# Compressive memory of a four-layer attention kernel, kept as two row halves of four heads each

## The chip, the core and the metric

The kernel runs on one core of one Trainium2 chip. The metric is the device time of one execution in microseconds (us). A core has five engines with queues of their own that meet only through semaphores: TensorE (PE, with its weight loads shown apart as PEld), VectorE (DVE), ScalarE (ACT), GpSimd (POOL) and SyncE (SP), which issues most DMA transfers. Matrix products read SBUF and write banks of PSUM.

## The reference, cut to what matters

Four layers alternate over a sequence of 2048 tokens, width 512, 32 heads of 16: A (linear attention with a learned feature map), B (local attention in four segments of 512 tokens, plus a memory carried from segment to segment), A, B. The change lies in B's memory.

```python
for s in range(N):                                   # N = 4 segments
    qs, ks, vs = q[:, :, s], k[:, :, s], v[:, :, s]
    logits = einsum("bhqd,bhkd->bhqk", qs, ks) * scale + mask
    a_dot = einsum("bhqk,bhkd->bhqd", softmax(logits), vs)
    pq = phi(qs)                                     # phi(t) = t + 1 if t > 0 else exp(t)
    num = einsum("bhld,bhde->bhle", pq, M)
    den = einsum("bhld,bhd->bhl", pq, z)[..., None] + 1e-6
    outs.append(g * num / den + (1.0 - g) * a_dot)   # g = sigmoid(beta), one per head
    pk = phi(ks)
    M = M + einsum("bhld,bhle->bhde", pk, vs)
    z = z + einsum("bhld->bhd", pk)
```

`M` is 16 x 16 for each head and `z` one column of 16. The kernel keeps both side by side as 17 columns (`VW` = 17), the last one being `z`.

## The kernel before, in words

**Layer B in chunks and steps.** A segment `s` is worked in four chunks `c` of eight heads (128 rows of features). Each chunk is two halves `m` of four heads, and each `m` takes five steps, so a layer has 160 steps `k`. A step emits, in this order: the logits of `attend` (tile `lg`, two row halves of 64 at array position (64e, 0), line 1096), the logits for the row maxima in `maxima` (tiles `mx` and `my`, row halves too, line 1054), then what earlier steps put off, with the weighted sums `pv` in two of five steps, and last the words of a table.

**The tables.** `FIRST`, `GAPS`, `LAST` and `FINAL` (lines 52 to 101) say by hand which work stands in which step: `4.1` is step 1 of half 4 of a segment. `a1` is the first generator step of `memory` for chunk 1 (the read), `t1` and `m1` its transposition and its sum; `max` is `put_maxima` (a transposition of the maxima into a bank, a copy `mt` by ACT, and a DMA into row 63 of Q); `fin` transposes the weighted sums `U` and normalises them; `q`, `k`, `v`, `out` are projections of 12 products of 128x512. A `+` means the next segment, `~` that the low part is put off to a later step. PE's program order is exactly the order of emission (`held`, line 173), and so is that of DVE, ACT, POOL and SP, save for a few instructions.

**Banks.** All of these write the tile `g`, of which there are three banks (`G` = 3, line 33). A bank is used again when its last reader is done.

**The memory.** For a chunk, `acc` and `kn` are 128 rows by 8 heads x 17 columns: every row of features against all eight heads, of which only the head's own block counts. `kn` is `acc` times the 0/1 pattern `bdB` and the gate (both on POOL). The read (`a`, from segment 1 on) takes two generator steps of two products each: `ph` (512 tokens) as weights in 128x128 pieces, `kn` as the moving 128x136, then `weigh` on DVE: add 1e-6, reciprocal, multiply. The sum (`m`, up to segment 2) takes four accumulated products of 128x128 weights `pk` with 128x136 of `v`, and DVE adds the bank to `acc`. Each product in plain f32 runs as two passes, each with a weight load of its own: 4 reads are 8 passes.

The read happens for 3 segments x 4 chunks x 2 layers = 24 times, and so does the sum.

Of the kernel before, what the change touches and what calls it, by code (L numbers as in the profile page):

```python
# [7 lines left out]
F32 = mybir.dt.float32  # L8
# [9 lines left out]
DH = 16  # L18
P = 128
NSEG = 4  # L20
NC = D // P
NT = T // P
VW = DH + 1
# [9 lines left out]
G = 3  # L33
# [17 lines left out]

FIRST = """
0.1 max k2/2       | 0.2 v3/2          | 0.3 k2~
0.4 v3             | 1.1 max m0 q3/2   | 1.3 fin q3~       | 1.4 t1 k3/1
2.1 max m1 k3      | 2.3 fin ln~       | 2.4 ln~ ln~
3.3 fin q0+/2      | 3.0 w
3.1 max ln~        | 3.4 q0+~ t2
4.1 max k0+/2 load | 4.3 fin k0+/1     | 4.4 k0+ m2
5.0 n              | 5.3 fin q1+/2 n
5.1 max v0+        | 5.4 q1+~ t3  # L60
6.1 max a0+ v1+    | 6.2 n             | 6.3 a0+ fin k1+/2
6.4 k1+ m3         | 7.0 n             | 7.2 n
7.1 max q2+~       | 7.3 fin v2+/2 n   | 7.4 v2+ t0+
"""
GAPS = """
0.2 n              | 0.3 a1 fin v3/3 n
0.1 max a1 k2~     | 0.4 v3 turn~ m0
1.0 n              | 1.2 n
1.1 max q3~        | 1.3 fin out/2     | 1.4 out t1 turn~
2.1 max a2 m1 k3~  | 2.3 fin ln out/3  | 2.4 out turn~ ln  # L70
3.1 max ln ln out~ | 3.3 a2 fin q0+/2  | 3.4 q0+~ t2
4.1 max k0+~ a3 turn~ load | 4.3 a3 fin out/3 | 4.4 out~ m2
5.0 n              | 5.3 fin v0+/2 n N
5.1 max q1+~ begin | 5.4 v0+ t3
6.0 N              | 6.1 max a0+ k1+~  | 6.2 n
6.3 a0+ fin v1+/3 N | 6.4 v1+ m3       | 7.0 n N
7.1 max q2+~       | 7.2 n N           | 7.3 fin v2+/2 n N
7.4 v2+ t0+
"""

LAST = """
0.1 max a1 k2~     | 0.2 n             | 0.3 a1 fin v3/3 n
1.0 n              | 0.4 v3 turn~      | 1.2 n
1.1 max q3~        | 1.3 fin out/2     | 1.4 out turn~
2.1 max k3~        | 2.3 fin a2 out/2  | 2.4 out a2 turn~
3.1 max ln~ ln~    | 3.3 fin out/2 ln~ | 3.4 out ln~ turn~
4.1 max v/2        | 4.3 fin out/2     | 4.4 out v
5.1 max v/2        | 5.3 fin v         | 5.4 a3 pre
6.1 max v/2        | 6.3 fin v a3      | 6.4 v/2 pt~
7.1 p v pt~        | 7.3 fin v/2 p pt  | 7.4 v p pt  # L90
"""
FINAL = """
0.1 max k2~        | 0.3 fin v3/3      | 0.4 v3 a1
1.1 max a1 q3/2    | 1.3 fin q3~       | 1.4 turn~
2.1 max k3/2       | 2.3 fin k3        | 2.4 out/2
3.1 max a2 out turn~ | 3.3 fin out/2   | 3.4 out~ a2
4.1 max a3 turn~   | 4.3 fin out/2     | 4.4 out/1 a3
5.1 max out turn~  | 5.3 fin out/2     | 5.4 out/1 pre
6.1 max out~       | 6.3 fin           | 6.4 pt~
7.1 p pt~          | 7.3 fin p pt      | 7.4 p pt  # L100
# [7 lines left out]
def interleave_kernel(ctx, tc, x_in, a_wqkv, a_wphi, a_wo, b_wq, b_wk, b_wv, b_wo, b_beta,  # L108
                      c_ident, c_mask, c_bd, out):
    nc = tc.nc  # L110
    MUL, ADD, SUB, MAX, MIN = ALU.mult, ALU.add, ALU.subtract, ALU.max, ALU.min

    cp = ctx.enter_context(tc.tile_pool(name="cp", bufs=1))
    wp = ctx.enter_context(tc.tile_pool(name="wp", bufs=4))
    hp_ = ctx.enter_context(tc.tile_pool(name="hp", bufs=2))
    sp = ctx.enter_context(tc.tile_pool(name="sp", bufs=2))
# [7 lines left out]
    def nm(s):  # L124
        uid[0] += 1
        return f"{s}_{uid[0]}"

    def T2(tag, bufs, dt=F32, shape=(P, 512)):
        return sp.tile(list(shape), dt, tag=tag, bufs=bufs, name=nm(tag))

    def PS(tag, bufs, shape=(P, 512)):
        return ps.tile(list(shape), F32, tag=tag, bufs=bufs, name=nm(tag))
# [38 lines left out]
    dve, act, pool, sync = [Ordered(e) for e in (nc.vector, nc.scalar, nc.gpsimd, nc.sync)]  # L171

    def held(i):

        if last[0] is not None:
            behind(i, last[0])
        last[0] = i
        return i
# [3 lines left out]
    def mm(*a, **k):  # L182
        n = a[0].free_size()
        work[0] += n / 2.26 if k["rhs"].dtype == F32R else (n * 2 / 2.4 + 25 if "tile_position" in k else 2 * max(112, n * 2 / 2.4))
        return held(nc.tensor.matmul(*a, **k))  # L185

    def tp(*a):
        work[0] += 108
        return held(nc.tensor.transpose(*a))  # L189

    def dma(out, in_):
        sync.dma_start(out=out.bitcast(F32), in_=in_.bitcast(F32))

    ident = cp.tile([P, P], F32, name="ident")
    bd = cp.tile([P, 27], F32, name="bd")
    bdA, bdB = bd[:, 0:8], bd[:, 8:16]
    mask = cp.tile([P, 512], F32, name="mask")
    gates = cp.tile([P, 2, H], F32, name="gates")
    eb = cp.tile([P, H], F32, name="eb")
# [280 lines left out]
    def weigh(out, p, eps, add, eng=pool):  # L480

        n, G = out.shape[1], out.shape[2]
        r = T2("r", 4, shape=(P, n, G))
        den = p[:, :, :, DH]
        if eps:
            dve.tensor_scalar(r, den, eps, None, op0=ADD)
            den = r
        dve.reciprocal(r, den)
        rb = r.unsqueeze(3).broadcast_to([P, n, G, DH])
        if not add:  # L490
            dve.tensor_tensor(out=out, in0=p[:, :, :, 0:DH], in1=rb, op=MUL)
            return
        t = T2("wt", 1, shape=(P, n, G, DH))
        dve.tensor_tensor(out=t, in0=p[:, :, :, 0:DH], in1=rb, op=MUL)
        eng.tensor_tensor(out=out, in0=out, in1=t, op=ADD)
# [433 lines left out]
    class LayerB:  # L929
# [4 lines left out]
            self.later, self.late, self.rows, self.turned = [], [], [], []  # L934

        def start(self):
            self.mem = sp.tile([P, NC, 2, 8 * VW], F32, tag="acc", bufs=1, name=nm("mem"))
            self.sets = []
            for b in range(NSET):
                Q, K = [T2("e8", 2 * NSET, F32R, (P, 4, 512)) for _ in range(2)]  # L940
                self.sets.append((Q, K))
                for t, rows in ((Q, mask[0:32, 0:P]), (K, ones)):
                    dma(t[3:P:4].rearrange("p a t -> p (a t)"), rows.unsqueeze(1).broadcast_to([32, 16, P]))
                    yield
# [46 lines left out]
            return self.ot[s, c]  # L991

        def memory(self, s, c):
            d = self.st[s, c]
            acc, kn = [self.mem[:, c, a] for a in range(2)]
            if s > 0:
                ph = d["phi", 0]
                ot = self.sums(s, c).rearrange("p q (h d) -> p q h d", d=DH)
                for a in range(2):
                    pn = PS("g", G)  # L1000
                    for q in range(2):
                        mm(pn[:, q * 8 * VW : (q + 1) * 8 * VW],
                                         lhsT=ph[:, (2 * a + q) * P : (2 * a + q + 1) * P], rhs=kn,
                                         start=True, stop=True)
                    weigh(ot[:, 2 * a : 2 * a + 2], pn[:, 0 : 16 * VW].rearrange("p (q h e) -> p q h e", q=2, h=8),
                          1e-6, False)
                    yield
            if s < NSEG - 1:
                ph = d["phi", 1]
                pt = PS("g", G)  # L1010
                for t in range(4):
                    tp(pt[:, t * P : (t + 1) * P], ph[:, t * P : (t + 1) * P], ident)
                pk = T2("tb3", 2)
                act.copy(pk, pt)
                yield
                v = self.vv[s][0]
                pm = PS("g", G)
                for t in range(4):
                    mm(pm[:, 0 : 8 * VW], lhsT=pk[:, t * P : (t + 1) * P],
                                     rhs=v[:, t, c * 8 * VW : (c + 1) * 8 * VW], start=(t == 0), stop=(t == 3))  # L1020
                if s == 0:
                    dve.tensor_copy(acc, pm[:, 0 : 8 * VW])
                else:
                    dve.tensor_tensor(out=acc, in0=pm[:, 0 : 8 * VW], in1=acc, op=ADD)
                pool.tensor_tensor(out=kn.rearrange("p (h e) -> p h e", e=VW),
                                        in0=acc.rearrange("p (h e) -> p h e", e=VW),
                                        in1=bdB.unsqueeze(2).broadcast_to([P, 8, VW]), op=MUL)
                kv = kn.rearrange("p (h e) -> p h e", e=VW)[:, :, 0:DH]
                pool.tensor_tensor(out=kv, in0=kv, op=MUL,
                                        in1=gates[:, 1, 8 * c : 8 * c + 8].unsqueeze(2).broadcast_to([P, 8, DH]))  # L1030
                yield

        def stack(self, m):
# [319 lines left out]
    for i in range(2):  # L1353
        lb = LayerB(xs[2 * i + 1], xs[2 * i + 2])
        run(p1[i])
        a2 = la[i].pass2()
# [40 lines left out]
```

## Time and profile before

| | |
|---|---|
| median of 3 runs | 1477.33 us (1476.87 to 1477.45) |
| the profiled execution's own time | 1477.91 us |
| its span, first to last instruction | 1476.2 us |
| granted TensorE clock, mean | 0.999 |
| PE | 97% busy, 10888 matmul passes |
| DVE, ACT, POOL | 74%, 53%, 44% busy |

A PE row of a timeline gives the start of the first pass of a run, the time to the end of its last, and their count. Passes are pipelined, so ends overlap the next start; what a pass costs is read from start to start. `128*64 128x68` is a weight tile of 128 rows by 64 columns and a moving operand of 128 by 68. In brackets stands the idle time before a row and what ended it. Engine and line are followed by the tiles, out<-in.

### The profile page before, as it was taken

Reading aid. Unit: us, or ns where it says so; the run is one execution under the profiler, and the core shown is the slowest. Engines: PE = TensorE matmul, PEld = TensorE weight load, DVE = VectorE, ACT = ScalarE, POOL = GpSimd, SP = SyncE. Lnnn points to the kernel's source line nnn. Section 1 sums busy time; section 2 is a strip of 40 time slices with the busy share of each in tenths; the row PEclk is TensorE's granted clock in tenths of the full one; section 3 lists DMA queues with packets and bytes.
Section 4 is the critical chain, followed back from the end, with each engine's and each line's share of the span. In section 5 each row is a group of like instructions: output and inputs, shape, how many; then the busy total and the mean of one; then the engine's idle time right before and its main releaser. Section 6 shows DMA issues by size and latency. Waiting matters only on the chain.

```text
span 1476.2 us, 30336 instructions
## 1 busy us (share of the span) xinstructions
PE 1436.9 (97%) x10888; PEld 1028.2 (70%) x10888; DVE 1094.6 (74%) x3258; ACT 785.4 (53%) x1178; POOL 649.9 (44%) x1000
## 2 busy tenths in 40 slices
PE   7999999999999999999999999999999999999997
PEld 6887878765666666666578887886566666666664
DVE  4766787778877877878656777868787787787783
ACT  5555345446665565565544334552665655656553
POOL 1668654224444544333324446540444445534331
PEclk9999999999999999999999999999999999999999
DMA  5387275545334434545340104764453453343330
GB/s 189 115 315 267 68 250 175 159 127 177 110 106 135 120 95 119 140 102 147 112 150 24 57 30 159 240 185 118 129 167 101 110 150 94 108 130 96 85 109 37
DMA packets 108773, 195.85 MB, mean 133 GB/s; under 512 B 14416, under 2 KB 27856, under 8 KB 107856
## 3 DMA queue, kind: packets, MB, share of 16 engines
q1 hardware_dynamic: 107472, 193.38, 43.9%
q8 instruction: 88, 1.44, 0.4%
q10 hardware_dynamic: 1152, 0.52, 0.1%
q14 instruction: 61, 0.50, 0.1%
HBM read 101.05 MB, written 39.85 MB: 95 GB/s over the span
## 4 chain that ended last, share of the span: by engine, by line
PE 72%; DVE 11%; ACT 3%; issue 2%; POOL 0%; POOLq 0%; ACTq 0%; DVEq 0%
PE g L185 40%; PE pv L185 9%; PE lg L185 8%; PE g L189 5%; PE mx L185 5%; PE my L185 3%; DVE mx L163 2%; DVE my L163 1%; PE lg L189 1%; DVE es L163 1%; ACT P L163 1%; DVE mxs L163 1%; DVE tmp L163 1%; DVE ol L163 1%; DVE rr L163 1%
## 5 line engine op out<-in xcount | busy, mean ns | idle before, releaser
L163 ACT ACTIVATE P<-lg 128x1024 f32<-128x1024 f32 x320 | 329.1, 1028 | 173.7 <-PE lg L185 164.2
L163 POOL TENSOR_SCALAR_AFFINE_SELECT P<-P 128x256 f32<-128x256 f32 (+1 forms) x448 | 190.4, 439 | 449.2 <-ACT P L163 448.6
L163 DVE CUSTOM_DVE_ANT_0 mx<-mx,mask 128x128 f32<-128x128 f32 (+3 forms) x512 | 255.3, 499 | 151.3 <-PE my L185 109.8
L163 DVE CUSTOM_DVE_ANT_0 my<-my,mask 128x128 f32<-128x128 f32 (+3 forms) x512 | 265.8, 519 | 6.5
L185 PE MATMUL g<-hh,wqk 128*128 128x512 f32 x512 | 180.3, 407 | 0.7 <-ACT mt L163 0.7
L185 PE MATMUL lg<-e,e 64*128 64x256 f32 (+2 forms) x1024 | 168.1, 386 | 2.8 <-ACT P L163 2.7
L185 PE MATMUL g<-w,oh 128*128 128x512 f32 x512 | 169.5, 412 | 1.0 <-ACT oh L163 0.7
L185 PE MATMUL pv<-P,v 128*32 128x512 f32 (+3 forms) x2048 | 164.0, 438 | 0.0
L185 PE MATMUL my<-e,e 63*128 63x256 f32 (+2 forms) x512 | 146.5, 346 | 6.9 <-DVE mxs L163 5.7
L185 PEld LDWEIGHTS lg<-e,e 64*128 64x128 f32 x1024 | 81.0, 184 | 97.8 <-issue 52.3
L185 PE MATMUL g<-w,hh 128*128 128x512 f32 x448 | 145.8, 406 | 0.0
L163 DVE DVE_READ_ACCUMULATOR2_ANT mxs<- 128x1 f32 x1024 | 145.1, 142 | 0.0
L185 PE MATMUL mx<-e,e 63*128 63x256 f32 (+2 forms) x512 | 140.4, 329 | 0.4
L185 PEld LDWEIGHTS pv<-P,v 128*32 128x32 f32 x2048 | 53.6, 109 | 100.0 <-issue 90.4
L185 PEld LDWEIGHTS g<-hh,wqk 128*128 128x128 f32 x512 | 96.3, 188 | 22.3 <-ACT mt L163 1.1
L185 PEld LDWEIGHTS g<-w,oh 128*128 128x128 f32 x512 | 88.8, 189 | 23.2 <-issue 2.6
L185 PE MATMUL g<-w,ol 128*128 128x512 f32 x256 | 102.4, 400 | 0.0
L185 PE MATMUL g<-hl,wqk 128*128 128x512 f32 x256 | 100.1, 391 | 0.0
L163 ACT CAST ta<-g 128x512 fp32r<-128x512 f32 x64 | 37.6, 587 | 116.1 <-PE g L185 115.8
L185 PEld LDWEIGHTS my<-e,e 63*128 63x128 f32 x512 | 82.3, 185 | 20.7 <-DVE mxs L163 9.6
L185 PEld LDWEIGHTS mx<-e,e 63*128 63x128 f32 x512 | 90.0, 186 | 6.0 <-DVE mxs L163 1.8
L163 POOL TENSOR_SCALAR tb<-tb 128x512 f32<-128x512 f32 x48 | 71.4, 1487 | 50.1 <-ACT tb L163 49.2
(155 smaller groups left out, 2801.2 us busy)
## 6 DMA issues: line engine op xcount, KB each, us to landing
e<-ta SPq DMA_DIRECT2D x384, 128.0 KB
wqk<-wqk SPq DMA_DIRECT2D x64, 512.0 KB
x<-x SPq DMA_DIRECT2D x48, 256.0 KB
ot<-in SPq DMA_DIRECT2D x28, 256.0 KB
pq<-tb SPq DMA_DIRECT2D x24, 256.0 KB
tb<-pq SPq DMA_DIRECT2D x24, 256.0 KB
x<-xr SPq DMA_DIRECT2D x24, 256.0 KB
xr<-x SPq DMA_DIRECT2D x24, 256.0 KB
```

Of the source, the lines that this page charges most:

```text
L163: i = f(*a, **k)
L185: return held(nc.tensor.matmul(*a, **k))
L189: return held(nc.tensor.transpose(*a))
```

## The change

The memory of a chunk becomes 128 rows by 4 heads x 17 columns (`mem` halves, from 136 to 68 columns). Rows 0 to 63 hold heads 0 to 3 of the chunk and rows 64 to 127 heads 4 to 7. The read becomes eight products in row halves (64x128 weights, 64x68 moving) into two banks, in one generator step; the sum becomes eight products in column halves (128x64 weights, 128x68 moving) into the two row halves of one bank. The pattern `bdB` gets four columns; the gating on POOL becomes two instructions of 64 rows.

In the tables each read is now one word instead of two and stands first in its step, ahead of `max`; `m0` and `m1` of some steps move behind the projection of their step.

```diff
 FIRST
-0.4 v3             | 1.1 max m0 q3/2   | 1.3 fin q3~       | 1.4 t1 k3/1
-2.1 max m1 k3      | 2.3 fin ln~       | 2.4 ln~ ln~
+0.4 v3             | 1.1 max q3/2 m0   | 1.3 fin q3~       | 1.4 t1 k3/1
+2.1 max k3 m1      | 2.3 fin ln~       | 2.4 ln~ ln~
...
-6.1 max a0+ v1+    | 6.2 n             | 6.3 a0+ fin k1+/2
+6.1 a0+ max v1+    | 6.2 n             | 6.3 fin k1+/2
 GAPS
-0.2 n              | 0.3 a1 fin v3/3 n
-0.1 max a1 k2~     | 0.4 v3 turn~ m0
+0.2 n              | 0.3 fin v3/3 n
+0.1 a1 max k2~     | 0.4 v3 turn~ m0
...
-2.1 max a2 m1 k3~  | 2.3 fin ln out/3  | 2.4 out turn~ ln
-3.1 max ln ln out~ | 3.3 a2 fin q0+/2  | 3.4 q0+~ t2
-4.1 max k0+~ a3 turn~ load | 4.3 a3 fin out/3 | 4.4 out~ m2
+2.1 a2 max k3~ m1  | 2.3 fin ln out/3  | 2.4 out turn~ ln
+3.1 max ln ln out~ | 3.3 fin q0+/2  | 3.4 q0+~ t2
+4.1 a3 max k0+~ turn~ load | 4.3 fin out/3 | 4.4 out~ m2
...
-    bd = cp.tile([P, 27], F32, name="bd")
-    bdA, bdB = bd[:, 0:8], bd[:, 8:16]
+    bd = cp.tile([P, 31], F32, name="bd")
+    bdA, bdB = bd[:, 0:8], bd[:, 27:31]
...
-            self.mem = sp.tile([P, NC, 2, 8 * VW], F32, tag="acc", bufs=1, name=nm("mem"))
+            self.mem = sp.tile([P, NC, 2, 4 * VW], F32, tag="acc", bufs=1, name=nm("mem"))
...
             acc, kn = [self.mem[:, c, a] for a in range(2)]
+            halves = [slice(64 * e, 64 * e + 64) for e in range(2)]
             if s > 0:
                 ph = d["phi", 0]
                 ot = self.sums(s, c).rearrange("p q (h d) -> p q h d", d=DH)
-                for a in range(2):
-                    pn = PS("g", G)
-                    for q in range(2):
-                        mm(pn[:, q * 8 * VW : (q + 1) * 8 * VW],
-                                         lhsT=ph[:, (2 * a + q) * P : (2 * a + q + 1) * P], rhs=kn,
-                                         start=True, stop=True)
-                    weigh(ot[:, 2 * a : 2 * a + 2], pn[:, 0 : 16 * VW].rearrange("p (q h e) -> p q h e", q=2, h=8),
-                          1e-6, False)
-                    yield
+                pn = [PS("g", G) for _ in halves]
+                for q in range(4):
+                    for e, rows in enumerate(halves):
+                        mm(pn[e][:, q * 4 * VW : (q + 1) * 4 * VW], lhsT=ph[rows, q * P : (q + 1) * P], rhs=kn[rows],
+                           start=True, stop=True, tile_position=(64 * e, 0))
+                for e in range(2):
+                    weigh(ot[:, :, 4 * e : 4 * e + 4],
+                          pn[e][:, 0 : 16 * VW].rearrange("p (q h e) -> p q h e", q=4, h=4), 1e-6, False)
+                yield
...
-                pm = PS("g", G)
+                pm = PS("g", G)[:, 0 : 4 * VW]
                 for t in range(4):
-                    mm(pm[:, 0 : 8 * VW], lhsT=pk[:, t * P : (t + 1) * P],
-                                     rhs=v[:, t, c * 8 * VW : (c + 1) * 8 * VW], start=(t == 0), stop=(t == 3))
+                    for e, rows in enumerate(halves):
+                        mm(pm[rows], lhsT=pk[:, t * P + 64 * e : t * P + 64 * e + 64],
+                           rhs=v[:, t, (8 * c + 4 * e) * VW : (8 * c + 4 * e + 4) * VW],
+                           start=(t == 0), stop=(t == 3), tile_position=(0, 64 * e))
                 if s == 0:
-                    dve.tensor_copy(acc, pm[:, 0 : 8 * VW])
+                    dve.tensor_copy(acc, pm)
                 else:
-                    dve.tensor_tensor(out=acc, in0=pm[:, 0 : 8 * VW], in1=acc, op=ADD)
-                pool.tensor_tensor(out=kn.rearrange("p (h e) -> p h e", e=VW),
-                                        in0=acc.rearrange("p (h e) -> p h e", e=VW),
-                                        in1=bdB.unsqueeze(2).broadcast_to([P, 8, VW]), op=MUL)
-                kv = kn.rearrange("p (h e) -> p h e", e=VW)[:, :, 0:DH]
-                pool.tensor_tensor(out=kv, in0=kv, op=MUL,
-                                        in1=gates[:, 1, 8 * c : 8 * c + 8].unsqueeze(2).broadcast_to([P, 8, DH]))
+                    dve.tensor_tensor(out=acc, in0=pm, in1=acc, op=ADD)
+                kn = kn.rearrange("p (h e) -> p h e", e=VW)
+                pool.tensor_tensor(out=kn, in0=acc.rearrange("p (h e) -> p h e", e=VW),
+                                   in1=bdB.unsqueeze(2).broadcast_to([P, 4, VW]), op=MUL)
+                for e, rows in enumerate(halves):
+                    kv = kn[rows, :, 0:DH]
+                    pool.tensor_tensor(
+                        out=kv, in0=kv, op=MUL,
+                        in1=gates[rows, 1, 8 * c + 4 * e : 8 * c + 4 * e + 4].unsqueeze(2).broadcast_to([64, 4, DH]))
                 yield
```

`LAST` and `FINAL` change in the same way: the second word of each read goes, the first moves to the head of a step `.1`.

More of the change, by code (lines that the diff above doesn't have):

```diff
@@ L65 @@
 GAPS = """
-0.2 n              | 0.3 a1 fin v3/3 n
-0.1 max a1 k2~     | 0.4 v3 turn~ m0
+0.2 n              | 0.3 fin v3/3 n
+0.1 a1 max k2~     | 0.4 v3 turn~ m0
 1.0 n              | 1.2 n
 1.1 max q3~        | 1.3 fin out/2     | 1.4 out t1 turn~
-2.1 max a2 m1 k3~  | 2.3 fin ln out/3  | 2.4 out turn~ ln
-3.1 max ln ln out~ | 3.3 a2 fin q0+/2  | 3.4 q0+~ t2
-4.1 max k0+~ a3 turn~ load | 4.3 a3 fin out/3 | 4.4 out~ m2
+2.1 a2 max k3~ m1  | 2.3 fin ln out/3  | 2.4 out turn~ ln
+3.1 max ln ln out~ | 3.3 fin q0+/2  | 3.4 q0+~ t2
+4.1 a3 max k0+~ turn~ load | 4.3 fin out/3 | 4.4 out~ m2
 5.0 n              | 5.3 fin v0+/2 n N
 5.1 max q1+~ begin | 5.4 v0+ t3
-6.0 N              | 6.1 max a0+ k1+~  | 6.2 n
-6.3 a0+ fin v1+/3 N | 6.4 v1+ m3       | 7.0 n N
+6.0 N              | 6.1 a0+ max k1+~  | 6.2 n
+6.3 fin v1+/3 N | 6.4 v1+ m3       | 7.0 n N
 7.1 max q2+~       | 7.2 n N           | 7.3 fin v2+/2 n N
@@ L81 @@
 LAST = """
-0.1 max a1 k2~     | 0.2 n             | 0.3 a1 fin v3/3 n
+0.1 a1 max k2~     | 0.2 n             | 0.3 fin v3/3 n
 1.0 n              | 0.4 v3 turn~      | 1.2 n
 1.1 max q3~        | 1.3 fin out/2     | 1.4 out turn~
-2.1 max k3~        | 2.3 fin a2 out/2  | 2.4 out a2 turn~
+2.1 a2 max k3~     | 2.3 fin out/2     | 2.4 out turn~
 3.1 max ln~ ln~    | 3.3 fin out/2 ln~ | 3.4 out ln~ turn~
-4.1 max v/2        | 4.3 fin out/2     | 4.4 out v
-5.1 max v/2        | 5.3 fin v         | 5.4 a3 pre
-6.1 max v/2        | 6.3 fin v a3      | 6.4 v/2 pt~
+4.1 a3 max v/2     | 4.3 fin out/2     | 4.4 out v
+5.1 max v/2        | 5.3 fin v         | 5.4 pre
+6.1 max v/2        | 6.3 fin v         | 6.4 v/2 pt~
 7.1 p v pt~        | 7.3 fin v/2 p pt  | 7.4 v p pt
@@ L92 @@
 FINAL = """
-0.1 max k2~        | 0.3 fin v3/3      | 0.4 v3 a1
-1.1 max a1 q3/2    | 1.3 fin q3~       | 1.4 turn~
+0.1 max k2~        | 0.3 fin v3/3      | 0.4 v3
+1.1 a1 max q3/2    | 1.3 fin q3~       | 1.4 turn~
 2.1 max k3/2       | 2.3 fin k3        | 2.4 out/2
-3.1 max a2 out turn~ | 3.3 fin out/2   | 3.4 out~ a2
-4.1 max a3 turn~   | 4.3 fin out/2     | 4.4 out/1 a3
+3.1 a2 max out turn~ | 3.3 fin out/2   | 3.4 out~
+4.1 a3 max turn~   | 4.3 fin out/2     | 4.4 out/1
 5.1 max out turn~  | 5.3 fin out/2     | 5.4 out/1 pre
@@ L1375 @@
     p = np.arange(P)
-    bd = np.zeros((P, 27), np.float32)
+    bd = np.zeros((P, 31), np.float32)
     bd[[16, 33, 80, 97], 26] = 0.5e-6
@@ L1381 @@
     bd[p, p // 32] = 1.0
-    hb = p // 64 * 4 + (p % 2) * 2 + p // 32 % 2
-    bd[p, 8 + hb] = 1.0
+    bd[p, 27 + (p % 2) * 2 + p // 32 % 2] = 1.0
     ins = [np.ascontiguousarray(np.asarray(A_x)[0]), A_wqkv, A_w_phi, A_wo, B_wq, B_wk, B_wv, B_wo, B_beta,
```

## The prediction

> **What bounds the kernel now.** I read the page first (busy times, then the chain of waits), then the windows over layer B, then PE's timeline around a few reads and sums.
>
> ```profile
> PE 1436.9 (97%) x10888; PEld 1028.2 (70%) x10888; DVE 1094.6 (74%) x3258; ACT 785.4 (53%) x1178; POOL 649.9 (44%) x1000
> PE 72%; DVE 11%; ACT 3%; issue 2%; POOL 0%; POOLq 0%; ACTq 0%; DVEq 0%
> ```
>
> PE carries the chain, but 97% is an average. This window of 90 us lies in the stage that the change touches (PE busy and its passes, then the other engines):
>
> ```profile
> core 0: us, PE busy (x) PEld busy (x) DVE busy (x) ACT busy (x) POOL busy (x), PEclk, DMA share, GB/s
> 380.00:470.00 90.00, 89.43 (x658) 59.86 (x659) 70.13 (x251) 55.40 (x82) 39.87 (x69) 1.00 0.40 107
> ```
>
> PE is idle for 0.6 us of these 90, at the full clock. So a step's length is what PE issues in it, and time that PE gains or loses there goes straight into the end: there is no idle time to swallow it. I therefore cost the change in starts of PE passes, never in their durations, which overlap.
>
> ```profile
> L185 PE MATMUL g<-mem,tb x192: 277/279/384, 383.1 to 1426.2; 128*128 128x136 f32 x192
> L163 POOL TENSOR_TENSOR mem<-mem,bd x24: 414/416/418, 321.8 to 1351.6; 128x136 f32<-128x136 f32 x24
> ```
>
> 192 read passes are 24 reads of 8; the 24 gatings on POOL say that there are 24 sums.
>
> **The sum in column halves: a gain.** A sum at the end of a step:
>
> ```profile
> 365.86 0.40 PE L185 MATMUL g<-hh,wqk 128*128 128x512 f32 x1
> 366.09 1.09 PE L185 MATMUL g<-v,tb 128*128 128x136 f32 x8
> 367.11 0.50 PE L185 MATMUL lg<-e,e 64*128 64x512 f32 x2
> ```
>
> The end of a step without one:
>
> ```profile
> 386.31 0.39 PE L185 MATMUL g<-w,hl 128*128 128x512 f32 x1
> 386.63 0.57 PE L185 MATMUL lg<-e,e 64*128 64x256 f32 x4
> ```
>
> From the last projection product to the logits it is 1.25 us with a sum (365.86 to 367.11) and 0.32 without, so a sum costs 0.93. The new form, 128x64 weights and 68 moving columns in two column halves, already runs in layer A:
>
> ```profile
> 216.81 1.17 PE L185 MATMUL g<-KN,P 128*64 128x68 f32 x32
> 217.91 1.09 PE L189 MATMUL lg<-ident,P 128*128 128x128 f32 x8
> ```
>
> 32 passes take 1.10 us, with the way out of the column arrangement in it. Such a change costs about 0.10: 0.32 from a product to the logits against 0.23 between products (365.86 to 366.09). So 16 passes take half of 1.00, plus 0.10 for the way out, 0.60; the way in is the 0.32 that stands there anyway. Gain 0.33 a sum, between 0.28 (16 passes at 0.55 and 0.10) and 0.43 (0.50 flat). Where `m0` or `m1` trades places with a projection, the same changes are paid in another order. **24 x 0.33 = 7.9 us gained** (6.7 to 10.3).
>
> **The read in row halves: nothing gained in the products.** What decides is how fast 64x68 passes can follow each other, which no row shows. Weight loads (busy us, mean ns):
>
> ```profile
> L185 PEld LDWEIGHTS lg<-e,e 64*128 64x128 f32 x1024 | 81.0, 184 | 97.8 <-issue 52.3 <-ACT P L163 42.4 <-ACT mt L163 0.4
> L185 PEld LDWEIGHTS g<-KN,P 128*64 128x64 f32 x1024 | 33.3, 137 | 10.1 <-ACT P L163 5.4 <-issue 3.5 <-DVE ot L163 0.3
> L185 PEld LDWEIGHTS g<-mem,tb 128*128 128x128 f32 x192 | 26.3, 190 | 4.6 <-issue 3.7
> ```
>
> And two products in row halves:
>
> ```profile
> 387.03 0.40 PE L185 MATMUL mx<-e,e 63*128 63x512 f32 x1
> 387.04 0.39 PE L185 MATMUL my<-e,e 63*128 63x512 f32 x1
> ```
>
> A load's time goes with its columns (137 ns for 64, 190 for 128: 0.83 ns a column, so 0.106 us for 128 from load to load), while 64 rows take what 128 take (184, 190). The sum's new weights have half the columns; the read's keep all 128. Two row halves do run beside each other (`mx` and `my` start 0.01 apart). So a pair of half passes costs about 0.115, what one full pass costs (366.09 to 367.11 less the change, by 8), and eight pairs replace eight passes. Bounds: 0.0625 a pair, layer A's pace (1.00 by 16), if the load doesn't bind; 0.115 a single half pass if the halves don't overlap. I take 0.115.
>
> The Trainium skill speaks against the read here ("TensorE: Matmul & The Clock Gate", section "LDWEIGHTS (loading the stationary operand)"): the load time follows the columns and not the rows of the contraction, at 1.2 columns a ns. The three load rows agree; by its figure a pair would cost 0.107 (an estimate from that page), 1.5 us less over the 24 reads.
>
> **The read in one step: a new wait.** The read's first half now:
>
> ```profile
> 410.99 0.34 PE L185 MATMUL my<-e,e 63*128 63x384 f32 x1
> 411.26 0.28 PE L189 MATMUL g<-ident,mxs 128*16 128x128 f32 x1
> ...
> 412.08 0.40 PE L185 MATMUL g<-hl,wqk 128*128 128x512 f32 x1
> ```
>
> The second half, ahead of a `fin`, and then a `fin` without a read:
>
> ```profile
> 417.22 0.33 PE L185 MATMUL my<-e,e 63*128 63x384 f32 x1
> 417.48 0.73 PE L185 MATMUL g<-mem,tb 128*128 128x136 f32 x4
> 418.05 0.60 PE L189 MATMUL g<-ident,U 128*128 128x128 f32 x4
> ...
> 403.49 0.34 PE L185 MATMUL my<-e,e 63*128 63x384 f32 x1
> 403.79 0.66 PE L189 MATMUL g<-ident,U 128*128 128x128 f32 x4
> ```
>
> Second half out: from `my` to the end of the `U` run 1.43 against 0.96, **0.47 saved**. The second fin starts as soon as PE is free, so `U` isn't late without the cover (if it were, a part of the 0.47 is lost). First half: from the last `my` to the second projection product it is 1.09 now (410.99 to 412.08). Afterwards the read takes two of the three banks at once, the maxima's transposition takes the third, and the projection behind it needs a fourth. In the changed program's instruction order, with its waits, that projection waits in 23 of 24 reads for `mt`, ACT's copy out of the transposition's bank; before, the first half read used that time. PE's order is fixed, so lg, mx, my and pv of all later steps queue behind it. The trace has this very wait, in the lead-in of a layer, and further on the same pair without it:
>
> ```profile
> 288.61 0.28 PE L189 MATMUL g<-ident,mxs 128*16 128x128 f32 x1 [0.86 <-DVE xr L163]
> 289.24 0.50 PE L185 MATMUL g<-hh,wqk 128*128 128x512 f32 x1 [0.35 <-ACT mt L163]
> 289.58 0.39 PE L185 MATMUL g<-hl,wqk 128*128 128x512 f32 x1
> ...
> 398.00 0.28 PE L189 MATMUL g<-ident,mxs 128*16 128x128 f32 x1
> ...
> 398.34 0.39 PE L185 MATMUL g<-hl,wqk 128*128 128x512 f32 x1
> ```
>
> ACT and DVE in the step of the read at 410.99:
>
> ```profile
> 410.97 1.02 ACT L163 ACTIVATE P<-lg 128x1024 f32<-128x1024 f32 x1 [0.76 <-PE lg L185]
> ...
> 413.53 0.42 DVE L163 TENSOR_TENSOR ot<-g,r 128x256 f32<-128x256 f32 x1
> ```
>
> Transposition to second product: 0.97 with the wait, 0.34 without. In the lead-in no exponential stood in ACT's way, so 0.97 is the shortest path; nor will one here: it ends at 411.99, and the transposition would start at 412.12 (410.99 + 0.17 + 0.80 + 0.16, worked out next). Sum from `my`: 0.17 into the read (384 columns at 0.23 for 512, no change of arrangement, since `my` runs in row halves too; between 0.11 and the 0.27 seen to the transposition), 7 x 0.115 = 0.80, way out 0.16 (68 two-cycle columns 0.06, change 0.10), 0.97: 2.10, against 1.09. **+1.01, less 0.47: +0.54 a read, 23 x 0.54 = 12.4**; the 24th, without the wait, gives 0.54 - 0.63 = -0.09. Reads: **+12.3 us**.
>
> Off the path: DVE adds and POOL gates half the columns (414 to 418 ns now on POOL); both have room (70 and 40 of 90 us busy). A second gating instruction costs POOL at most as much as the one it is split from. DVE's two weighings now come in a row; the one above ends 2.96 after `my`, a second needs about 0.9, so 3.9; the next taker of their banks comes after 2.10 + 10 x 0.23 = 4.4. That is covered; uncovered it would be PE's wait. The mask of `bd` and the DMAs of `max` stay, about a microsecond later, with four steps in hand.
>
> **Sum.** 1477.91 (own time of the profiled execution) - 7.9 + 12.3 = 1482.3. The runs shown have a median 0.58 lower, so 1481.7, say **1482 us**, 0.3% slower.
>
> **Rivals.**
>
> *Row halves pay in full.* At 0.0625 a pair a read saves 7 x 0.0525 = 0.37, 24 times 8.8: 1473, faster. For it: layer A's pairs. Against it: those loads have 64 columns. It decides from a pace under about 0.09. The Trainium skill says this much too ("TensorEngine Tiling (Array Packing)", section "Theoretical Speedup"): up to twice the speed for a dimension of 64. Its rule holds in the rows of layer A for columns; no row here shows it for 68 moving columns in row halves.
>
> *The wait is cheaper,* because the change doesn't do what the program's waits say, or because the stall takes another's place: without it 0.63 x 23 = 14.5 go, down to 1467; with half of it, 1475. Against it: two rows with it, and PE has no other idle time here.
>
> *Halves run one after the other.* 15 x 0.115 in place of 0.80 is 0.93 a read, 22 us: 1504. Against it: `mx` and `my`.
>
> **Chances.** Forecast 0.62 (1478 to 1487); row halves pay 0.12; cheaper wait 0.13; no overlap 0.06; mixtures 0.07. Range **1471 to 1488**: it takes in the first rival and half of the second. A measurement of this kernel can tell 0.2%, 3 us, from no change. Slower (over 1480.3): 0.56 of the forecast's 0.62, and the third rival, together 0.62. Faster (under 1474.4): 0.09 of the first rival, 0.08 of the second, 0.04 of the mixtures, together 0.21. Same: the rest, 0.17.
>
> **What will show it.** In the changed profile: 16 passes of `g<-v,tb` with about 0.6 from the first to the logits; read passes in pairs 0.115 apart; `PE g <- ACT mt` with some 23 waits of 0.35; and `fin` right behind `my`. I am wrong if the pairs stand 0.06 apart, or if no row shows PE waiting for `mt`.

## The result, and the profile after

The changed kernel takes 1484.78 us (median of six runs, 1483.88 to 1485.26) beside 1477.56 for the kernel before (six runs): ratio 1.0046, 95% interval 1.0033 to 1.0059. It is slower by half a per cent, 2.8 us more than the 1482 forecast, and inside the range.

The page of the changed kernel: its span, then busy times, then the chain of waits by engine.

```profile
span 1483.0 us, 31120 instructions
...
PE 1432.0 (97%) x11272; PEld 1018.0 (69%) x11272; DVE 1092.9 (74%) x3258; ACT 788.2 (53%) x1178; POOL 652.8 (44%) x1024
...
PE 72%; DVE 10%; ACT 3%; issue 2%; POOL 1%; SPq 0%; DMA 0%; DVEq 0%; POOLq 0%; ACTq 0%
```

PE issues 384 passes more and is busy 4.9 us less, and yet the span is 6.8 us longer: most of what was added is waiting. The window of 90 us that starts at the same step as the one shown of before, with the columns named there:

```profile
377.36:467.36 90.00, 88.30 (x705) 58.58 (x707) 70.04 (x251) 55.81 (x82) 40.17 (x72) 1.00 0.41 107
```

PE's idle time went from 0.57 to 1.70 us at the same clock. The view of PE's waits in layer B's first pass (waiting engine and tile, releaser, us in total, times, longest) names it, with a row that the kernel before didn't have at all there:

```profile
PE g L185 <- ACT mt L163: 4.3, 12, 0.4
```

Over both passes 23 of the 24 reads have it, with 0.35 to 0.36 us each.

The read in PE's timeline, at the same step as the read at 410.99 of the prediction:

```profile
408.21 0.34 PE L185 MATMUL my<-e,e 63*128 63x384 f32 x1
408.28 1.12 PE L185 MATMUL g<-mem,tb 64*128 64x68 f32 x16
409.32 0.28 PE L189 MATMUL g<-ident,mxs 128*16 128x128 f32 x1
409.96 0.50 PE L185 MATMUL g<-hh,wqk 128*128 128x512 f32 x1 [0.36 <-ACT mt L163]
410.30 0.39 PE L185 MATMUL g<-hl,wqk 128*128 128x512 f32 x1
```

From the last `my` to the second projection product it is 2.09 us (408.21 to 410.30), where before it was 1.09: 0.07 into the read, 1.04 to the transposition, 0.64 with the wait for `mt`, 0.34. The read's second half is gone from the step two further on:

```profile
415.42 0.34 PE L185 MATMUL my<-e,e 63*128 63x384 f32 x1
415.73 0.66 PE L189 MATMUL g<-ident,U 128*128 128x128 f32 x4
416.14 0.71 PE L185 MATMUL g<-w,hh 128*128 128x512 f32 x2
```

And a sum (the one at 365.86 of before had one projection product ahead of it too):

```profile
391.47 0.40 PE L185 MATMUL g<-hh,wqk 128*128 128x512 f32 x1
391.80 0.69 PE L185 MATMUL g<-v,tb 128*64 128x68 f32 x16
392.43 0.50 PE L185 MATMUL lg<-e,e 64*128 64x512 f32 x2
```

0.96 from the product to the logits against 1.25 before: 0.33 into the column halves, 0.63 from the sum's first pass to the logits. By its own row the sum gained 0.29.

**The ledger.** I took the start of every step's logits in both traces and added the differences of the steps in which each part stands. The span grew by 6.9 (unrounded), in these parts:

| part | forecast, us | trace, us |
|---|---|---|
| 12 sums that stand in steps `.1` or `0.4` (`m0`, `m1`) | -4.0 | -3.4 |
| 12 sums at `4.4` and `6.4` (`m2`, `m3`), with the two steps behind them | -4.0 | -1.7 |
| 23 reads, with all that is left of layer B | +12.4 | +9.2 |
| the 24th read (steps `3.1` to `3.4` of the last segment) | -0.1 | +2.0 |
| two stretches of the changed kernel at half the clock | 0 | +3.0 |
| code that the change doesn't touch (layer A, the ends) | 0 | -2.2 |

The last row belongs to the one profiled execution of before: most traces below are 0.4 to 2 us ahead of it at the start of layer B too, in code that is the same in all of them.

The row on the clock comes from the windows of the changed kernel (columns as above):

```profile
725.50:728.90 3.40, 3.40 (x20) 2.12 (x13) 0.04 (x1) 1.17 (x2) 0.41 (x1) 0.50 0.89 271
1411.60:1415.00 3.40, 3.40 (x17) 2.13 (x20) 0.81 (x2) 1.06 (x2) 0.00 (x0) 0.50 0.21 75
```

The granted clock stood at 0.50 for 3.4 us twice, and the passes of the steps there took 1.5 us longer each time. In layer B the trace of before has no such stretch. The first stands in steps `6.0` and `6.1` of the first pass's last segment; three other traces below have one there too, seven have none, and its cause stays open. The second follows the stall of the 24th read, which is told further down.

### The profile page after: what moved, and what is told of

Its sections match the earlier page's. It is cut to its first block, busy times and chain, and to the rows that moved or that the text cites. A ratio compares the mean times of both kernels' runs of the same rounds, so it can differ in the third digit from the quotient of the medians.

```text
span 1483.0 us, 31120 instructions
## 1 busy us (share of the span) xinstructions
PE 1432.0 (97%) x11272; PEld 1018.0 (69%) x11272; DVE 1092.9 (74%) x3258; ACT 788.2 (53%) x1178; POOL 652.8 (44%) x1024
## 4 chain that ended last, share of the span: by engine, by line
PE 72%; DVE 10%; ACT 3%; issue 2%; POOL 1%; SPq 0%; DMA 0%; DVEq 0%; POOLq 0%; ACTq 0%
PE g L185 39%; PE pv L185 9%; PE lg L185 9%; PE g L189 5%; PE mx L185 5%; PE my L185 3%; DVE mx L163 2%; PE lg L189 1%; DVE my L163 1%; DVE es L163 1%; ACT P L163 1%; DVE mxs L163 1%; DVE tmp L163 1%; POOL P L163 1%; DVE ol L163 1%
## 5 line engine op out<-in xcount | busy, mean ns | idle before, releaser
L185 PEld LDWEIGHTS g<-w,hh 128*128 128x128 f32 x448 | 79.6, 190 | 19.6 <-ACT mt L163 1.6
```

## The experiments

The experiments take the prediction's terms one at a time. The rivals for the missing 3 us: sums that don't gain where they stand, and a read that loses elsewhere.

### The sums alone

The tables and the read of before; only the sum in column halves, with POOL spreading it back to eight heads.

```diff
-                    mm(pm[:, 0 : 8 * VW], lhsT=pk[:, t * P : (t + 1) * P], ...)
+                    for e in range(2):
+                        mm(pm[64 * e : 64 * e + 64], lhsT=pk[:, t * P + 64 * e : t * P + 64 * e + 64], ...,
+                           tile_position=(0, 64 * e))
```

> The tables and the read of before (full products, two steps), and only the sums in column halves; GpSimd spreads the four columns back over eight heads. Theory (sums gain, reads lose): a sum costs 0.62 us in place of 0.93, 24 x 0.31 = 7.4 less than before: 1470 us. Rival (the halves gain nothing once they stand in place, or GpSimd's spreading makes the next read late): 1477 or more.

1475.57 us (before 1477.50), ratio 0.9987, interval 0.9978 to 0.9997: a gain of some 2 us, not the 7.4 expected. The steps show two reasons. Eight sums stand between full-array products here, pay a change of arrangement on the way in and another on the way out, and gain only 0.11; in the changed kernel's tables they stand last in their step, and gain 0.30. And twelve sums, those of steps `4.4` and `6.4`, make their step 0.30 shorter and the next one 0.30 longer.

### The reads alone

The changed kernel with the sums as full products; DVE then adds each row half by an instruction of its own.

```diff
-                    for e, rows in enumerate(halves):
-                        mm(pm[rows], lhsT=pk[:, t * P + 64 * e : t * P + 64 * e + 64], ...)
+                    mm(pm[:, 0 : 8 * VW], lhsT=pk[:, t * P : (t + 1) * P], ...)
...
+                for e, rows in enumerate(halves):
+                    dve.tensor_tensor(out=acc[rows], in0=pm[rows, 4 * e * VW : 4 * (e + 1) * VW], in1=acc[rows], op=ADD)
```

> The changed kernel with its sums by full products again; DVE copies or adds the two own blocks. Theory: the reads alone lose what the total lost and the sums' gain besides, 7.2 + 7.4 = 14.6 over before: 1492 us. Rival (what was lost comes from the sums' new places in the tables): 1478 to 1485.

1492.58 us, ratio 1.0103 (1.0088 to 1.0118): as expected, the loss lies with the reads. It overstates them a little: the three steps from each of the twelve sums in `4.4` and `6.4` on are 1.6 us longer in all than before, though PE's products there are the old ones. The sums have two adds on DVE here, which is the likely reason, since the next fences show DVE to set the pace in these steps.

The same two steps, `4.4` and `5.0`, in four kernels: the logits that start step `4.4`, the sum if one stands there, the logits of `5.0` and of `5.1`. PE's timeline of the kernel before:

```profile
482.01 0.50 PE L185 MATMUL lg<-e,e 64*128 64x256 f32 x4
...
483.49 1.09 PE L185 MATMUL g<-v,tb 128*128 128x136 f32 x8
484.50 0.50 PE L185 MATMUL lg<-e,e 64*128 64x512 f32 x2
...
486.40 0.50 PE L185 MATMUL lg<-e,e 64*128 64x512 f32 x2
```

Of the changed kernel:

```profile
479.65 0.50 PE L185 MATMUL lg<-e,e 64*128 64x256 f32 x4
...
481.22 0.69 PE L185 MATMUL g<-v,tb 128*64 128x68 f32 x16
481.84 0.50 PE L185 MATMUL lg<-e,e 64*128 64x512 f32 x2
482.18 0.40 PE L185 MATMUL mx<-e,e 63*128 63x512 f32 x1
482.40 0.50 PE L185 MATMUL my<-e,e 63*128 63x512 f32 x1
...
484.05 0.50 PE L185 MATMUL lg<-e,e 64*128 64x512 f32 x2
```

With a full sum the pair of steps lasts 4.39 us (482.01 to 486.40), with the cheaper one 4.40. Most of the 0.3 comes back between `mx` and `my`, which in the kernel before start together in this step and here stand 0.22 apart. No idle time is recorded, since the recorded passes overlap.

### Two ways around the wait for `mt`

First: the maxima's transposition goes ahead of the read, so that the read's products cover ACT's copy.

```diff
-2.1 a2 max k3~ m1
+2.1 max a2 k3~ m1
```

> The changed kernel with the transposition of the maxima ahead of the read again in all steps with a read. Theory (the wait for the copy of the maxima is the loss): the copy runs under the read, 23 waits and the 2 us stall at 1407 go, and two more changes of the array's arrangement come, about 0.3 us a read: 0.2 less a read, 1478 us (1475 to 1481), and no wait of PE for mt in these steps. Rival (the change of arrangement costs more than the wait): 1487 or more.

1481.94 us, ratio 1.0032 (1.0021 to 1.0043): better than the change by 2.8 us, not by 7. The row of waits for `mt` is gone. But the read now takes the second and third bank behind the transposition, and at eight sites the second bank isn't free:

```profile
380.02 0.69 DVE L163 TENSOR_TENSOR ta<-g,ta 128x512 fp32r<-128x512 f32 x1 [0.51 <-ACT tb L163]
```

```profile
380.25 1.61 PE L185 MATMUL g<-mem,tb 64*128 64x68 f32 x16
381.80 0.50 PE L185 MATMUL g<-w,hh 128*128 128x512 f32 x1
```

These are DVE's and PE's timelines at the read of step `6.1`: 1.55 from the read to the projection, where run and way out take 1.04. DVE is emptying a projection's bank until 380.71. The wait moved from one bank to another.

Second: the transposition writes into the free end of the read's second bank (272 of 512 columns are in use), and DVE's weighing is put behind it. The read then needs no third bank, and the projection no fourth.

```diff
+            self.room = pn[1]
+            yield
             for e in range(2):
                 weigh(ot[:, :, 4 * e : 4 * e + 4], ...)
...
-            pt = PS("g", G)
-            tp(pt[0:16, 0:P], self.mx.pop(m), ident)
+            pt = (self.room if self.room is not None else PS("g", G))[0:16, 512 - P : 512]
+            tp(pt, self.mx.pop(m), ident)
```

> The changed kernel, order of PE kept, but the maxima are transposed into the free end of the read's second bank, so the projection finds the third bank free; DVE's weighing comes behind the copy. Theory (three banks for four takers): 23 x 0.62 and the 2 us stall go: 1468 us. Rival (the time is spent in PE's products, or another wait, for DVE's weighing or the next bank, takes its place): 1478 to 1485.

1468.67 us, ratio 0.9941 (0.9927 to 0.9956): as expected, and faster than the kernel before. PE's timeline at the same step:

```profile
380.07 0.33 PE L185 MATMUL my<-e,e 63*128 63x384 f32 x1
380.14 1.11 PE L185 MATMUL g<-mem,tb 64*128 64x68 f32 x16
381.18 0.28 PE L189 MATMUL g<-ident,mxs 128*16 128x128 f32 x1
381.21 0.70 PE L185 MATMUL g<-w,hh 128*128 128x512 f32 x2
```

The transposition is followed by the projection after 0.03 us instead of 0.64, and the read itself is unchanged. 23 x 0.61 = 14.0, and 16.1 were gained between the medians, 17.6 between the two traces. In the traces the rest is the 3.0 of the two stretches at half the clock, which are not there, and 1.5 of the 24th read, whose stall shrinks to 0.6, less 1.2 that four later steps give back. This is the change with its one new wait taken away in 23 reads, and settles what that wait cost.

### The read in quarters

Each row-half product is split once more, into two column halves, so that a weight load has 64 columns and not 128.

```diff
-                        mm(pn[e][:, q * 4 * VW : ...], lhsT=ph[rows, q * P : (q + 1) * P], rhs=kn[rows], ...)
+                        for j in (0, 64):
+                            mm(pn[e][j : j + 64, q * 4 * VW : ...], lhsT=ph[rows, q * P + j : q * P + j + 64],
+                               rhs=kn[rows], ..., tile_position=(64 * e, j))
```

> The changed kernel with each read product also cut in column halves (weights 64x64, two halves of the tokens beside each other), so four products run at a time. Theory (the pace of a read is that of a load of 128 columns, 0.11 us): loads of 64 columns go at layer A's 0.059, eight groups take 0.47 in place of 0.84 us, 24 x 0.37 = 8.9 less: 1476 us. Rival (something else sets the pace, the issue of passes or the change of arrangement): no gain, 1484 or more.

1482.25 us, ratio 1.0032 (1.0021 to 1.0042): 2.5 us under the change where 8 to 9 were expected.

```profile
381.99 0.33 PE L185 MATMUL my<-e,e 63*128 63x384 f32 x1
382.25 0.70 PE L185 MATMUL g<-mem,tb 64*64 64x68 f32 x32
382.98 0.28 PE L189 MATMUL g<-ident,mxs 128*16 128x128 f32 x1
383.61 0.73 PE L185 MATMUL g<-w,hh 128*128 128x512 f32 x2 [0.36 <-ACT mt L163]
```

The products did what was expected: from the first start to the last it is 0.485 us, groups of four 0.059 apart, against 0.845 and pairs 0.112 apart. But `my` runs in row halves, so the way in now has a change of arrangement: 0.26 instead of 0.07, and the way out is no cheaper in this row (0.25). From `my` to the transposition it is 0.99, against 1.11 in the changed kernel: 0.1 of the 0.36 is left. This row is one of six with a way out of about 0.25; at most other reads it is 0.15, and 0.2 is left. Added up, the steps of the 23 reads are 4.5 us shorter in this trace, of 8.9 expected. The medians show 2.5; in the traces the other 2.0 are lost ahead of layer B, in code that is the same in both. With the shared bank as well:

> Quarters and the shared bank together. Theory (two separate prices): 1468.7 - 8.9 = 1460 us. Rival (they are the same idle time seen twice): 1468 or more.

1466.43 us, ratio 0.9921 (0.9907 to 0.9936), the fastest version found. Again the quarters bring some 2 us (2.2 between the medians), not 8.9.

### Where the sums stand

If DVE sets the length of the pair `.4` and `.0`, sums moved out of it should free nothing there. I had expected the opposite, that PE would save its 0.3 twelve times in another place:

```diff
-4.4 out~ m2
+4.4 out~
...
-5.1 max q1+~ begin
+5.1 max q1+~ m2 begin
```

> The shared bank, and the sums m2 and m3 moved from steps .4 to the next steps .1. Theory (the 0.3 us that a sum gains in a step .4 is given back in the step .0 behind it, where the product my waits for DVE's reductions of the step before): ten to twelve give-backs of 0.3 go, 1468.7 - 3 = 1465.5 us, and the steps .0 are as short as in the kernel before. Rival (the give-back has another cause, or DVE is late in the steps .1 too): 1468 to 1469.

1475.59 us, ratio 0.9985 (0.9976 to 0.9994): 6.9 us slower than the shared bank alone. PE's timeline of the same two steps, with no sum in them, and then DVE's:

```profile
479.02 0.50 PE L185 MATMUL lg<-e,e 64*128 64x256 f32 x4
...
480.64 0.50 PE L185 MATMUL lg<-e,e 64*128 64x512 f32 x2
480.98 0.40 PE L185 MATMUL mx<-e,e 63*128 63x512 f32 x1
481.77 0.50 PE L185 MATMUL my<-e,e 63*128 63x512 f32 x1 [0.39 <-DVE mxs L163]
...
483.41 0.50 PE L185 MATMUL lg<-e,e 64*128 64x512 f32 x2
```

```profile
481.22 0.43 DVE L163 CUSTOM_DVE_ANT_0 my<-my,mask 128x256 f32<-128x256 f32 x1
481.57 0.14 DVE L163 DVE_READ_ACCUMULATOR2_ANT mxs<- 128x1 f32 x1
```

The pair still lasts 4.39 us (479.02 to 483.41). Now the cause has become large enough for a row of its own: `my` of step `5.0` needs the bank that DVE is reducing for step `4.4`, whose last instruction ends at 481.71. So with 1.01, 0.62 or 0 us of sum in it, the pair is as long as DVE makes it. A sum there costs nothing, and in step `5.1` it costs its 0.6 nearly in full (0.5 to 0.6 by the steps): 12 x 0.6 = 7.2, near the 6.9 measured. All three edits together miss for the same reason:

> Quarters, shared bank and moved sums. Theory (three separate prices): 1468.7 - 8.9 - 3 = 1457 us. Rival: DVE becomes the bound of the steps of the reads, 1462 or more.

1473.47 us, ratio 0.9965 (0.9952 to 0.9978), 7.0 above the quarters with the shared bank.

The converse, with and without the quarters: the eight `m0` and `m1` that stand in steps `.1` go into a step `.4`.

```diff
-2.1 a2 max k3~ m1  | 2.3 fin ln out/3  | 2.4 out turn~ ln
+2.1 a2 max k3~     | 2.3 fin ln out/3  | 2.4 out turn~ ln m1
```

> The shared bank (1468.7), with the converse move: the eight sums m0 and m1 that stand in steps .1 (m0 and m1 of segment 0, m1 of segments 1 and 2, in two layers) go into the next or last step .4, ahead of a step .0. Theory A: the pair of steps .4 and .0 lasts what DVE needs, so PE has some 0.5 to 0.6 us to spare in it wherever it holds no sum; the eight sums then cost nothing there and save 0.6 each in steps .1: 8 x 0.6 = 4.8 less, 1464 (1463 to 1466). Rival B: only the pairs with m2 and m3 are DVE's (their other work decides); elsewhere PE sets the length of .4 and .0 too, the sums cost the same 0.6 in either place, 1468 to 1470. The steps .0 behind the moved sums tell: longer under B by what the step .4 gains, unchanged in their pair's sum under A.

> The same move in the version with the read in quarters and the shared bank (1466.4). Theory A: 1461.6 (1460.5 to 1463.5). Rival B: 1466 to 1468.

1476.31 us (ratio 0.9984, 0.9976 to 0.9993) and 1470.89 (0.9960, 0.9946 to 0.9973): slower than without the move by 7.6 and 4.5, which neither theory had allowed for. PE's timeline at step `2.4` of the first of them:

```profile
450.68 0.60 PE L189 MATMUL g<-ident,ot 128*128 128x128 f32 x4
451.11 0.60 PE L189 MATMUL g<-ident,x 128*128 128x128 f32 x4
452.50 0.69 PE L185 MATMUL g<-v,tb 128*64 128x68 f32 x16 [0.79 <-DVE xr L163]
```

The step has a projection, two runs of transpositions and then the sum: four takers of three banks, and the sum waits until DVE has emptied the projection's. Steps `4.4` and `6.4` have one projection ahead of the sum and no such wait. Step by step the eight sites lose 5.2 us in the first of them; the rest of its 7.6 doesn't lie in these steps. Two of the eight, `m0` in step `0.4` of segment 0, wait for ACT's copy of `v` instead. So the free time in steps `.4` is shown for `m2` and `m3` alone, and of the places tried the sums stood in the cheapest.

## Why the prediction was right, and where it was off

**The read's wait** was the step on which the sign hung, and it held: 2.10 forecast from `my` to the second projection product, 2.09 measured, with 0.36 of recorded idle for `mt` where 0.35 was quoted. The shared bank, which removes that wait in all 23 reads with PE's products and their order unchanged, turns the loss into a gain of 8.8 us on the kernel before. The rival of a cheaper wait is refuted by it.

**The pace of the products** held too: 0.115 a pair forecast, 0.112 measured. Halves run beside each other, which refutes the rival of 1504; and they don't pay in full, which refutes that of 1473, since each pass still loads 128 columns. The quarters show that condition: at 64 columns the pace is 0.059. The Trainium skill's rule that a load goes by its columns ("TensorE: Matmul & The Clock Gate", section "LDWEIGHTS (loading the stationary operand)") gives 0.107 and 0.053 as estimates, and the two paces lie 0.005 and 0.006 above them. The ways in and out were 0.07 and 0.20 against 0.17 and 0.16, and cancel with a run of 0.84 instead of 0.80.

**The second half** saved 0.45 to 0.53 at most sites, as forecast. At six it saved 0.73 to 0.77: before, the projection behind `U` also came late, likely by a wait for a bank, 0.61 from the transposition to it (418.05 in the prediction's fence, with the projection at 418.66) against 0.41 now. The prediction counted only to the end of the `U` run. 6 x 0.27 = 1.6 is half of the 3.2 by which the row of the 23 reads came out lower. Another 0.5 lies in steps `2.4` and `3.0` of segment 0, which hold no read; the rest is spread over many steps, and its cause stays open.

**The sums' 7.9 is a term that was mis-sized**: 5.1 were gained. "Time that PE gains or loses there goes straight into the end" was read from a window that is 99% busy, and is wrong for the pairs `4.4` and `5.0`, `6.4` and `7.0`. A busy PE is one whose recorded passes overlap, and up to 0.3 us of waiting hides under that. Ten of the twelve pairs gained 0.03 to 0.11 each in three steps, about what DVE's add got shorter (0.30 to 0.23), and two in segment 0 gained 0.4.

**The 24th read** was forecast at -0.1 because the projection doesn't wait for `mt` there. What does wait is the transposition. The prediction had DVE's weighing covered because the next taker of the read's banks was to come 4.4 us after `my`; here the transposition is that taker, and comes at once. PE's and then DVE's timeline of the changed kernel:

```profile
1407.58 1.01 PE L185 MATMUL g<-mem,tb 64*128 64x68 f32 x16
1410.61 0.27 PE L189 MATMUL g<-ident,mxs 128*16 128x128 f32 x1 [2.03 <-DVE r L163]
1410.64 0.71 PE L185 MATMUL g<-w,oh 128*128 128x512 f32 x2
...
1411.42 0.89 PE L185 MATMUL g<-w,oh 128*128 128x512 f32 x2
1412.11 0.63 PE L185 MATMUL g<-w,ol 128*128 128x512 f32 x1
```

```profile
1409.55 0.17 DVE L163 TENSOR_SCALAR r<-g 128x16 f32<-128x16 f32 x1
1409.76 0.25 DVE L163 RECIPROCAL r<-r 128x16 f32<-128x16 f32 x1
1410.04 0.42 DVE L163 TENSOR_TENSOR tmp<-g,r 128x256 f32<-128x256 f32 x1
```

A projection spread over several steps (`out`) holds the third bank, so the transposition needs one of the read's two, and gets it when the first weighing is done, behind DVE's reductions: 2.30 us from the read's last pass instead of 0.20. That is +2.1, and with the -0.1 the +2.0 of the ledger. Behind the stall comes the second stretch at half the clock: from 1411.42 to the next product it is 0.69 for two passes, where the kernel before has 0.46. All three traces with this stall (this one, the reads alone, the quarters) have such a stretch, which begins 1.9 to 3.3 us after the read's last pass, and none of the nine others has one at this place. That the stall brings it on is likely by this, and not shown. In the version with the shared bank the transposition follows after 0.20 here as well, and only a later run of transpositions waits for DVE, 0.6.

So the errors are +2.8 (sums), -3.2 (reads), +2.1 (24th read) and +3.0 (clock): their sum, 4.7, less the 2.2 by which the trace of before was slow elsewhere, is the difference between the forecast +4.4 and the 6.9 of the spans. The direction came from the wait, as forecast; that the total came within 3 us is in part luck, since errors of about 3 us each went both ways.

## What to carry to other kernels

When two steps of work are merged, count the buffers that are open at once, and follow each next taker in program order: here one read in two banks cost more by a wait of 0.64 us for a third and fourth than cheaper products could give, and an unused end of a bank bought it back. Before a gain is multiplied by its sites, look at each kind of site for the engine that sets its pace, by the time from landmark to landmark and not by busy shares. Row halves alone did not speed up this read's short products, whose weight loads have 128 columns. Halving the columns did, from 0.84 to 0.49 us a read, but the neighbours run in another arrangement, and the changes took 0.15 to 0.25 of that back.

## What the runs showed of the hardware

Changes of array arrangement took back 0.15 to 0.25 us of the 0.36 that the read's products save in quarters. Into row halves from row halves it is 0.07 us (`my` to the read), into quarters 0.26: 0.19 for the change. The Trainium skill says that changing the tiling mode drains TensorE ("TensorEngine Tiling (Array Packing)", section "Key Properties"); these rows fit that and give the size of the way in. Which part of the 0.20 on the way out is the drain, and which the last passes, wasn't separated. Also not tried: both row halves of the read in one bank, and a fourth bank for `g`.
